# Key masks and row sums on ScalarE, four query loads on its queue, probabilities normalised later

## The chip, the cores and the metric

The kernel runs on one core of one Trainium2 chip. A core has TensorE (matrix products into PSUM), VectorE, ScalarE and GpSimd (all of which work on SBUF, and VectorE and ScalarE on PSUM too), and SyncE, whose queue issues most loads and stores; ScalarE's queue can issue them as well. The engines run side by side and wait for each other by semaphores; each works through its own queue in order. The metric is the time of one execution on the device, in microseconds (us), lower is better.

## What is computed

Three stages, the output of each being the input of the next. Inputs are fp32; q and k are drawn eight times as wide as written here.

```python
# 1. attention: B, H, S, D = 4, 8, 576, 64; keys and values are averaged in groups of 8 -> 72 of each
k_p = k.reshape(B, H, 72, 8, D).mean(axis=3)
v_p = v.reshape(B, H, 72, 8, D).mean(axis=3)
scores = matmul(q, k_p.T) / sqrt(D)
attn = exp(scores - max(scores));  attn = attn / (sum(attn) + 1e-9)
x = matmul(attn, v_p)                      # then (B, S, H*D) -> 2304 tokens x 512
# 2. four experts, each weighted by a token's probability
p = domain_probs / (domain_probs.sum(-1) + 1e-9)
x = sum over e of p[:, e] * (relu(x @ w1[e]) @ w2[e])      # 512 -> 1024 -> 512
# 3. gated layer
out = ((x @ g_w1) * (x @ g_w2) @ g_w3) @ g_wout            # 512 -> 1024 -> 1024 -> 512
```

## The kernel before

The 2304 tokens are cut into 18 query tiles of 128 rows (t = 0 to 17) and six blocks of three tiles. Products are split into a high and a low part (`hi_lo`, lines 178 to 180: ScalarE writes the rounded high part, another engine the remainder), and each product is three matmuls (`mm3`, line 173).

The program begins with a lead-in (list `lead`, lines 651 to 654): keys and values of the first batch are pooled, the first three query tiles scored, exponentiated, normalised, turned and attended, which gives the first block of x. Then expert 0 runs over all blocks in units of (block, 128 hidden columns), in `run_first` (line 1182): a unit's first product, and two units later its second. The rest of the attention is threaded between these units: `hooks[n]` is a list of pieces that is run in gap n, and a unit of the first block has two gaps (one behind its first product, one behind the second product of the unit two places back). The order of each engine's queue is the order in which the code writes its instructions (`manual_schedule`).

A tensor name in the rows is that of the tile: `ap` is the area of the attention's small tiles, `plain` another area (masked keys, probabilities), `stx...` are staging tiles of loads, `raw` weights as loaded, `w2h`/`w2l` an expert's second weights split, `g` the bank of a unit's product.

What the change touches:

- `load_k` (line 399) loads 128 pooled rows' worth of keys; chunks 1 and 3 of the first batch go through ScalarE's queue, all others through SyncE's.
- `pool_k` (line 411) sums each group of eight keys into `kp` and multiplies it by a mask of two columns (line 424) into `kb`, so that one product scores two heads. For the second batch (b = 1) chunks 0 to 3 are done by GpSimd in the lead-in (lines 421 to 424), chunk 4 by VectorE in gap 1. `make_kT` (line 433) turns `kb` on TensorE (line 438), in gaps 3 (chunks 0 to 2) and 4 (chunks 3 and 4); ScalarE evacuates (line 442).
- `load_qb` (line 473) loads a query tile from t = 3 on; a tile that lies in two batches, as t = 4 does, takes eight loads, four for each part (line 481). VectorE turns it (`make_qT`, line 499).
- `scores` (line 505) writes two banks per tile. From the end of the lead-in on, scores, turned keys and turned probabilities share two banks in turn (`spare[:2]`, line 1127).
- `exps` (line 517): VectorE takes the maximum (line 525); for t = 0, 1, 3, 4, 5 ScalarE does one exponential per head (line 528), eight for a tile, for the others VectorE subtracts first (line 530) and ScalarE does two (line 531).
- `sums` (line 534): VectorE sums the exponentials (line 537) and makes the reciprocal (lines 538, 539); `normalise` (line 541) multiplies, on GpSimd or VectorE. `attn_T` (line 544) turns the result on TensorE (line 551), ScalarE evacuates (line 557). `attend` (line 559) multiplies with the pooled values (line 566).
- `probs` (line 623) normalises the experts' probabilities on VectorE (lines 625 to 628), in gap 7; `turn_dp` (line 636) brings them into place, ScalarE evacuates (line 640); their first reader is `accumulate` (line 711), behind the first block's last unit.
- `Stream.fill` (lines 198, 200) issues the loads of weights on SyncE's queue.

The exponentials of t = 3 stand in gap 0, of t = 4 in gap 5, of t = 5 in gap 8, the turning of t = 3 in gap 7, of t = 4 in gap 10.

Of the kernel before, what the change touches and what calls it, by code (L numbers as in the profile page):

```python
# [8 lines left out]
F32 = mybir.dt.float32  # L9
F32R = mybir.dt.float32r  # L10
U32 = mybir.dt.uint32
AF = mybir.ActivationFunctionType
ALU = mybir.AluOpType
AX = mybir.AxisListType
# [3 lines left out]
def fused_kernel(  # L18
# [16 lines left out]
    nc = tc.nc  # L35
    PSUM = bass.MemoryType.PSUM

    B, H, S, D = q.shape
# [4 lines left out]
    P = 128  # L43
# [5 lines left out]
    TPB = BLK // P  # L49
# [6 lines left out]
    NCH = (NROW + P - 1) // P  # L56
# [4 lines left out]
    def segments(t0, n):  # L61
        done = 0
        while done < n:
            b, s = divmod(t0 + done, S)
            step = min(n - done, S - s)
            yield done, step, b, s
            done += step

    LAG = 2
    LEAD = 3  # L70
# [260 lines left out]
    with tc.manual_schedule():  # L331
# [3 lines left out]

        ap = Places(**packed(ap1, [
            ("at", (H // 2) * BLK * 4, 2), ("e", H * NK * 4, 3), ("kT", NCH * P * 4, 2), ("vp", H * D * 4, 2), ("qT", NP * P * 4, 1),
            ("kp", D * 4, 2), ("mx", H * 4, 2), ("sm", H * 4, 2), ("hm", NCH * H * 4, 1), ("mk", NCH * 2 * 4, 1),
            ("sp", NTILE * 4, 1)], 4 * XO),
            **packed(plain, [("kb", NCH * 2 * D * 4, 1)], PLAIN, WORK + XT))  # L340
        acc_d = dpool.tile([P, NTILE, DM], F32, tag="acc", name="acc")
# [11 lines left out]
        hm = ap.tile([P, NCH, H], F32, tag="hm", name="hm", bufs=1)  # L353
# [5 lines left out]
        mk = ap.tile([P, NCH, 2], F32, tag="mk", name="mk", bufs=1)  # L359
# [19 lines left out]
        def stage(*what):  # L379
            holds[what] = spots[kind_of(what)].pop(0)  # L380
            return holds[what]
# [15 lines left out]
        in_t, kb_t, kT_t, vp_t, qT_t, sc_t, e_t, sm_t, at_t = {}, {}, {}, {}, {}, {}, {}, {}, {}  # L397
# [13 lines left out]
        def pool_k(b, c, eng=nc.vector):  # L411
            if c == 0:
                kb_t[b] = ap.tile([P, NCH, 2, D], F32, tag="kb", name="kb", bufs=1)
            r, n = in_t.pop(("k", b, c))
            kp = ap.tile([P, D], F32, tag="kp", name="kp")
            if n < P and b == 0:
                nc.gpsimd.memset(kb_t[b][n:, c], 0.0)
            if eng is nc.vector:
                eng.tensor_reduce(kp[:n], r[:n, :].rearrange("p (r d) -> p d r", d=D), axis=AX.X, op=ALU.add)  # L419
            else:  # L420
                eng.tensor_tensor(r[:n, :256], r[:n, :256], r[:n, 256:], op=ALU.add)
                eng.tensor_tensor(r[:n, :128], r[:n, :128], r[:n, 128:256], op=ALU.add)
                eng.tensor_tensor(kp[:n], r[:n, :64], r[:n, 64:128], op=ALU.add)
            (eng if b == 1 else nc.gpsimd).tensor_tensor(kb_t[b][:n, c], kp[:n].unsqueeze(1).broadcast_to([n, 2, D]),
                                    mk[:n, c].unsqueeze(2).broadcast_to([n, 2, D]), op=ALU.mult)

# [2 lines left out]
        def turn_ident(pw, n):  # L429
            for _ in range(n):  # L430
                nc.tensor.transpose(pw[:, :P], ident, ident)

        def make_kT(b, g0, g1):
            if g0 == 0:
# [31 lines left out]
        def load_q(t):  # L466
# [3 lines left out]
                                  q[b, :, s:s + n, :].rearrange("h p d -> p h d"))  # L470
            in_t["q", t] = r

        def load_qb(t):

            r = stage("qb", t).rearrange("p x (h c) -> p (x h) c", c=4 * D)
            for off, n, b, s in segments(t * P, P):
                view = q[b].rearrange("(h g) (j a) d -> g j h (a d)", g=2, a=4)
                for g in range(2):
                    for m in range(2):
                        p0 = 64 * g + 32 * m + off // 4  # L480
                        nc.sync.dma_start(r[p0:p0 + n // 4, :, :7 * 32],
                                          view[g, s // 4:(s + n) // 4, :, 32 * m:32 * (m + 7)])
            in_t["qb", t] = r.rearrange("p h (a x) -> p h a x", a=4)[:, :, :, :32]

        def make_qT(t):
# [17 lines left out]
        G = H // 2  # L503
# [13 lines left out]
        def exps(t):  # L517
            e = ap.tile([P, H, NK], F32, tag="e", name="e", bufs=3)
            mx = ap.tile([P, H], F32, tag="mx", name="mx")
            for half, sc in enumerate(sc_t.pop(t)):  # L520
                s3 = sc[:, :2 * W].rearrange("p (g j) -> p g j", j=NK)
                m = mx[:, half * G:(half + 1) * G]
                eh = e[:, half * G:(half + 1) * G]
                alone = t < 2 * TPB and t != LEAD - 1
                nc.vector.tensor_reduce(m, s3, axis=AX.X, op=ALU.max, negate=alone)  # L525
                if alone:
                    for g in range(G):
                        nc.scalar.activation(eh[:, g], s3[:, g], AF.Exp, bias=m[:, g:g + 1])  # L528
                else:
                    nc.vector.tensor_tensor(eh, s3, m.unsqueeze(2).broadcast_to([P, G, NK]), op=ALU.subtract)  # L530
                    nc.scalar.activation(eh, eh, AF.Exp)
            e_t[t] = e

        def sums(t):

            sm_t[t] = ap.tile([P, H], F32, tag="sm", name="sm")
            nc.vector.tensor_reduce(sm_t[t], e_t[t], axis=AX.X, op=ALU.add)  # L537
            nc.vector.tensor_scalar(sm_t[t], sm_t[t], 1e-9, float(POOL), op0=ALU.add, op1=ALU.mult)
            nc.vector.reciprocal(sm_t[t], sm_t[t])

        def normalise(t, eng):
            eng.tensor_tensor(e_t[t], e_t[t], sm_t[t].unsqueeze(2).broadcast_to([P, H, NK]), op=ALU.mult)
# [62 lines left out]
        def do_qT(t):  # L605
            return [(("q" if t < LEAD else "qb", t), lambda: make_qT(t))] if t < NTILE else []

        def do_scores(t):
            return [(None, lambda: scores(t))]

        def do_exps(t):
            return [(None, lambda: exps(t))]

        def do_normalise(t, eng=nc.gpsimd):
            return [(None, lambda: sums(t)), (None, lambda: normalise(t, eng))]
# [18 lines left out]
        W0, W1 = 20, 22  # L634
# [7 lines left out]
        def warm(n):  # L642

            def f():
                warm_ps.append(bank("warm"))
                turn_ident(warm_ps[-1], n)
            return [(None, f)]

        k0, kT0, k1, kT1 = do_k(0), do_kT(0), do_k(1, 4), do_kT(1, 3)
        v0 = do_v(0, GP, GP, GP, GP, GP, VE)[:6] + [(None, lambda: pool_v_pe(0, 6))]  # L650
        lead = (warm(W0) + k0[:4] + kT0[:1] + k0[4:] + do_qT(0) + kT0[1:] + do_qT(1) + do_scores(0) + do_exps(0) + v0[:3]
                + do_qT(2) + do_scores(1) + do_exps(1) + do_scores(2) + do_normalise(0) + v0[3:4] + do_exps(2) + warm(W1) + [(None, turn_dp)]
                + v0[6:] + do_normalise(1) + v0[4:5] + weight(GP) + do_turn(0) + do_normalise(2, VE) + v0[5:6] + do_turn(1) + do_turn(2)
                + do_qT(3) + k1[:4] + do_attend(0) + weight(VE))

        hooks = [[] for _ in range(2 * FC * ATT_BLOCKS + 11)]
        hooks[1] = k1[4:]
        hooks[7] = [(None, probs)]
        hooks[2] = do_qT(TPB + 1)
        hooks[3] = kT1[:1]  # L660
        hooks[4] = kT1[1:]
# [855 lines left out]
```

## Time and profile before

| | us |
|---|---|
| three runs: median (lowest to highest) | 1151.28 (1150.27 to 1153.33) |
| the profiled execution, its own time | 1150.86 |
| its span in the trace, first to last instruction | 1149.1 |
| granted TensorE clock, mean | 1.000 |

Busy in the span: TensorE 99%, VectorE 69%, GpSimd 37%, ScalarE 32%. Times in the rows are us from the start of the span unless marked ns. A row of the timeline has start, length, engine, line of the code, operation, destination and sources, count, and in brackets how long the engine stood idle before it and what it then waited for. The ends of matmuls are modelled, since they are pipelined. Where an instruction waits for several others, the trace names the one that it takes for the last.

### The profile page before, as it was taken

The page shows a single profiled execution, that of the slowest core. Times are in us where ns is not written, and L with a number is a line of the kernel's source. Part 1 is how long each engine was busy: PE and PEld are TensorE (multiplying, and loading weights), DVE is VectorE, ACT ScalarE, POOL GpSimd, SP SyncE. Part 2 cuts the span into 40 slices and gives each one's busy share as a digit, 9 for nine tenths or more (in the row PEclk, how much of TensorE's full clock was granted, in tenths as well). Part 3 has the DMA queues.
Part 4 walks back from the last instruction along what each step waited for, and adds up shares of the span by engine and source line. Part 5 has one row for each costly group of instructions (what it writes and reads, how often), then busy time and mean ns, then how long its engine had stood idle before and what let it go on. Part 6 is the DMA issues. An engine that isn't in the chain of part 4 may idle for free.

```text
span 1149.1 us, 17172 instructions
## 1 busy us (share of the span) xinstructions
PE 1141.3 (99%) x5995; PEld 1033.7 (90%) x5995; DVE 797.4 (69%) x1458; ACT 371.5 (32%) x633; POOL 421.9 (37%) x390
## 2 busy tenths in 40 slices
PE   9999999999999999999999999999999999999998
PEld 7898888999989898989898989989889999999997
DVE  7876553867768598658679678877786675774554
ACT  5543433345413053504134421305353223230110
POOL 6874212424616166534436652515000111331211
PEclk9999999999999999999999999999999999999999
DMA  9955525345875825495944678785485175947341
GB/s 215 235 136 133 170 80 202 142 175 179 299 246 171 259 79 162 138 313 171 271 151 125 192 224 193 240 210 140 151 198 230 35 267 202 336 153 283 116 164 55
DMA packets 211473, 213.85 MB, mean 186 GB/s; under 512 B 86569, under 2 KB 166697, under 8 KB 211387
## 3 DMA queue, kind: packets, MB, share of 16 engines
q1 hardware_dynamic: 211099, 212.23, 59.3%
q8 instruction: 47, 0.77, 0.3%
q10 hardware_dynamic: 288, 0.52, 0.1%
q14 instruction: 39, 0.32, 0.1%
HBM read 140.87 MB, written 71.83 MB: 185 GB/s over the span
## 4 chain that ended last, share of the span: by engine, by line
PE 96%; DMA 2%; DVE 1%; ACT 0%; POOL 0%; issue 0%; SPq 0%; ACTq 0%; DVEq 0%; POOLq 0%
PE g L176 18%; PE g L174 18%; PE g L175 18%; PE s L176 13%; PE s L175 13%; PE s L174 13%; PE x_ps L566 1%; PE sc L512 1%; PE at_ps L551 1%; DMA stxl<-in_moe_w_dram 1%; DMA stxl<-in_k_dram 1%; DMA stxl<-in_q_dram 0%; DVE ap L419 0%; DVE ap L525 0%; DVE ap L537 0%; ACT ap L528 0%
## 5 line engine op out<-in xcount | busy, mean ns | idle before, releaser
L972 DVE TENSOR_TENSOR plain<-s,plain 128x384 f32<-128x384 f32 x300 | 158.4, 554 | 81.0 <-ACT plain L976 33.5
L180 POOL TENSOR_TENSOR round<-x5l,round 128x768 fp32r<-128x768 f32 x60 | 112.2, 1871 | 271.6 <-ACT round L179 254.6
L176 PE MATMUL s<-xo,wl 128*128 128x384 f32 x624 | 208.8, 335 | 0.0
L174 PE MATMUL s<-xo,wh 128*128 128x384 f32 x624 | 208.8, 335 | 0.0
L175 PE MATMUL s<-xo,wh 128*128 128x384 f32 x624 | 208.8, 335 | 0.0
L174 PE MATMUL g<-w2l,round 128*128 128x512 f32 x522 | 205.1, 393 | 0.8 <-POOL w2l L180 0.8
L176 PE MATMUL g<-w2h,round 128*128 128x512 f32 x522 | 204.0, 391 | 0.0
L175 PE MATMUL g<-w2h,round 128*128 128x512 f32 x522 | 203.8, 390 | 0.0
L174 PEld LDWEIGHTS s<-xo,wh 128*128 128x128 f32 x624 | 117.2, 188 | 0.5
L175 PEld LDWEIGHTS s<-xo,wh 128*128 128x128 f32 x624 | 117.2, 188 | 0.5
L176 PEld LDWEIGHTS s<-xo,wl 128*128 128x128 f32 x624 | 117.2, 188 | 0.0
L174 PEld LDWEIGHTS g<-w2l,round 128*128 128x128 f32 x522 | 98.1, 188 | 21.1 <-POOL w2l L180 1.1
L176 PEld LDWEIGHTS g<-w2h,round 128*128 128x128 f32 x522 | 98.0, 188 | 20.7
L175 PEld LDWEIGHTS g<-w2h,round 128*128 128x128 f32 x522 | 98.1, 188 | 19.4
L292 POOL TENSOR_TENSOR x5l<-x5l,x5h 128x256 uint32<-128x256 uint32 x80 | 60.4, 754 | 138.5 <-DVE x5h L291 133.0
L976 ACT ACTIVATE plain<-s 128x384 f32<-128x384 f32 x60 | 29.2, 487 | 230.9 <-PE s L176 195.2
L179 ACT ACTIVATE round<-x5l 128x768 fp32r<-128x768 f32 x60 | 50.9, 848 | 147.7 <-DVE x5l L1377 146.5
L180 POOL TENSOR_TENSOR round<-plain,round 128x768 fp32r<-128x768 f32 (+1 forms) x29 | 52.4, 1808 | 116.2 <-ACT round L179 65.4
L286 DVE TENSOR_SCALAR x5l<-x5h 128x256 uint32<-128x256 uint32 x80 | 51.9, 649 | 54.8 <-DMA gate<-x5l 30.9
L972 DVE TENSOR_TENSOR x5l<-s,plain 128x384 f32<-128x384 f32 x120 | 65.5, 555 | 23.6 <-PE s L176 17.0
L1215 ACT ACTIVATE plain<-plain 128x768 f32<-128x768 f32 x36 | 30.5, 849 | 112.7 <-DVE plain L972 112.7
L704 DVE SCALAR_TENSOR_TENSOR round<-g,round 128x384 fp32r<-128x384 f32 x48 | 26.4, 551 | 58.1 <-ACT round L703 58.0
(255 smaller groups left out, 2254.2 us busy)
## 6 DMA issues: line engine op xcount, KB each, us to landing
xo<-keptx SPq DMA_DIRECT2D x42, 768.0 KB
raw<-in_moe_w_dram SPq DMA_DIRECT2D x54, 256.0 KB
keptx<-xo SPq DMA_DIRECT2D x12, 768.0 KB
x5h<-in_moe_w_dram SPq DMA_DIRECT2D x128, 64.0 KB
x5h<-in_moe_w_dram SPq DMA_DIRECT2D x32, 256.0 KB
ob<-acc SPq DMA_DIRECT2D x24, 256.0 KB
kept<-xo SPq DMA_DIRECT2D x8, 768.0 KB
xo<-kept SPq DMA_DIRECT2D x8, 768.0 KB
```

Source lines behind the costliest of these rows:

```text
L174: nc.tensor.matmul(ps, lh, rl, start=first, stop=False)
L175: nc.tensor.matmul(ps, lh, rh, start=False, stop=False)
L176: nc.tensor.matmul(ps, ll, rh, start=False, stop=last)
L179: nc.scalar.activation(hi, src, AF.Copy)
L180: (lo_eng or nc.vector).tensor_tensor(lo, src, hi.bitcast(F32), op=ALU.subtract)
L286: nc.vector.tensor_scalar(au, h, 0x7FFFFFFF, None, op0=ALU.bitwise_and)
L292: nc.gpsimd.tensor_tensor(au, au, l, op=ALU.add)
L512: nc.tensor.matmul(sc[off:off + n, (hp % 2) * W:(hp % 2 + 1) * W], qT[:, hp, off:off + n], kT_t[b][:, hp * W:(hp + 1) * W], start=True, st ...
L704: nc.vector.scalar_tensor_tensor(hl, ps, 0.0, hh.bitcast(F32), op0=ALU.max, op1=ALU.subtract)
L972: nc.vector.tensor_tensor(to, one, two, op=ALU.add)
L976: nc.scalar.activation(x, product(j, A11, B11), AF.Copy)
L1215: nc.scalar.activation(r, r, AF.Relu)
```

## The change

ScalarE multiplies the first three chunks of the second batch's keys by their masks (six activations of 128x64 in gap 0, ahead of the scores of t = 3), in place of three multiplications by GpSimd; the pooled keys get four places instead of two. For t = 3, 4, 5 each exponential also writes its row sum (`accum_out`), and `sums` leaves VectorE's sum out; the sums get three places instead of two. Four of the eight loads of query tile 4, those of its second part, are issued from ScalarE's queue, behind the exponentials of t = 2 in the lead-in. `probs` moves from gap 7 to gap 13.

```diff
@@ -335,7 +335,7 @@
 
         ap = Places(**packed(ap1, [
             ("at", (H // 2) * BLK * 4, 2), ("e", H * NK * 4, 3), ("kT", NCH * P * 4, 2), ("vp", H * D * 4, 2), ("qT", NP * P * 4, 1),
-            ("kp", D * 4, 2), ("mx", H * 4, 2), ("sm", H * 4, 2), ("hm", NCH * H * 4, 1), ("mk", NCH * 2 * 4, 1),
+            ("kp", D * 4, 4), ("mx", H * 4, 2), ("sm", H * 4, 3), ("hm", NCH * H * 4, 1), ("mk", NCH * 2 * 4, 1),
             ("sp", NTILE * 4, 1)], 4 * XO),
             **packed(plain, [("kb", NCH * 2 * D * 4, 1)], PLAIN, WORK + XT))
         acc_d = dpool.tile([P, NTILE, DM], F32, tag="acc", name="acc")
@@ -421,6 +421,9 @@
                 eng.tensor_tensor(r[:n, :256], r[:n, :256], r[:n, 256:], op=ALU.add)
                 eng.tensor_tensor(r[:n, :128], r[:n, :128], r[:n, 128:256], op=ALU.add)
                 eng.tensor_tensor(kp[:n], r[:n, :64], r[:n, 64:128], op=ALU.add)
+            if b == 1 and c < NCH - 2:
+                kp_t[c] = kp
+                return
             (eng if b == 1 else nc.gpsimd).tensor_tensor(kb_t[b][:n, c], kp[:n].unsqueeze(1).broadcast_to([n, 2, D]),
                                     mk[:n, c].unsqueeze(2).broadcast_to([n, 2, D]), op=ALU.mult)
 
@@ -429,6 +432,12 @@
         def turn_ident(pw, n):
             for _ in range(n):
                 nc.tensor.transpose(pw[:, :P], ident, ident)
+
+        kp_t = {}
+
+        def mask_k(c):
+            for a in range(2):
+                nc.scalar.activation(kb_t[1][:, c, a], kp_t[c], AF.Copy, scale=mk[:, c, a:a + 1])
 
         def make_kT(b, g0, g1):
             if g0 == 0:
@@ -470,16 +479,25 @@
                                   q[b, :, s:s + n, :].rearrange("h p d -> p h d"))
             in_t["q", t] = r
 
+        rest_of_q = []
+
         def load_qb(t):
 
             r = stage("qb", t).rearrange("p x (h c) -> p (x h) c", c=4 * D)
-            for off, n, b, s in segments(t * P, P):
+
+            def part(eng, off, n, b, s):
                 view = q[b].rearrange("(h g) (j a) d -> g j h (a d)", g=2, a=4)
                 for g in range(2):
                     for m in range(2):
                         p0 = 64 * g + 32 * m + off // 4
-                        nc.sync.dma_start(r[p0:p0 + n // 4, :, :7 * 32],
-                                          view[g, s // 4:(s + n) // 4, :, 32 * m:32 * (m + 7)])
+                        eng.dma_start(r[p0:p0 + n // 4, :, :7 * 32],
+                                      view[g, s // 4:(s + n) // 4, :, 32 * m:32 * (m + 7)])
+
+            for k, seg in enumerate(segments(t * P, P)):
+                if k and t == TPB + 1:
+                    rest_of_q.append(lambda seg=seg: part(nc.scalar, *seg))
+                else:
+                    part(nc.sync, *seg)
             in_t["qb", t] = r.rearrange("p h (a x) -> p h a x", a=4)[:, :, :, :32]
 
         def make_qT(t):
@@ -524,8 +542,11 @@
                 alone = t < 2 * TPB and t != LEAD - 1
                 nc.vector.tensor_reduce(m, s3, axis=AX.X, op=ALU.max, negate=alone)
                 if alone:
+                    if t >= LEAD and half == 0:
+                        sm_t[t] = ap.tile([P, H], F32, tag="sm", name="sm")
                     for g in range(G):
-                        nc.scalar.activation(eh[:, g], s3[:, g], AF.Exp, bias=m[:, g:g + 1])
+                        more = dict(accum_out=sm_t[t][:, half * G + g:half * G + g + 1]) if t >= LEAD else {}
+                        nc.scalar.activation(eh[:, g], s3[:, g], AF.Exp, bias=m[:, g:g + 1], **more)
                 else:
                     nc.vector.tensor_tensor(eh, s3, m.unsqueeze(2).broadcast_to([P, G, NK]), op=ALU.subtract)
                     nc.scalar.activation(eh, eh, AF.Exp)
@@ -533,8 +554,9 @@
 
         def sums(t):
 
-            sm_t[t] = ap.tile([P, H], F32, tag="sm", name="sm")
-            nc.vector.tensor_reduce(sm_t[t], e_t[t], axis=AX.X, op=ALU.add)
+            if t not in sm_t:
+                sm_t[t] = ap.tile([P, H], F32, tag="sm", name="sm")
+                nc.vector.tensor_reduce(sm_t[t], e_t[t], axis=AX.X, op=ALU.add)
             nc.vector.tensor_scalar(sm_t[t], sm_t[t], 1e-9, float(POOL), op0=ALU.add, op1=ALU.mult)
             nc.vector.reciprocal(sm_t[t], sm_t[t])
 
@@ -649,13 +671,15 @@
         k0, kT0, k1, kT1 = do_k(0), do_kT(0), do_k(1, 4), do_kT(1, 3)
         v0 = do_v(0, GP, GP, GP, GP, GP, VE)[:6] + [(None, lambda: pool_v_pe(0, 6))]
         lead = (warm(W0) + k0[:4] + kT0[:1] + k0[4:] + do_qT(0) + kT0[1:] + do_qT(1) + do_scores(0) + do_exps(0) + v0[:3]
-                + do_qT(2) + do_scores(1) + do_exps(1) + do_scores(2) + do_normalise(0) + v0[3:4] + do_exps(2) + warm(W1) + [(None, turn_dp)]
+                + do_qT(2) + do_scores(1) + do_exps(1) + do_scores(2) + do_normalise(0) + v0[3:4] + do_exps(2) + [(None, lambda: rest_of_q.pop()())]
+                + warm(W1) + [(None, turn_dp)]
                 + v0[6:] + do_normalise(1) + v0[4:5] + weight(GP) + do_turn(0) + do_normalise(2, VE) + v0[5:6] + do_turn(1) + do_turn(2)
                 + do_qT(3) + k1[:4] + do_attend(0) + weight(VE))
 
         hooks = [[] for _ in range(2 * FC * ATT_BLOCKS + 11)]
         hooks[1] = k1[4:]
-        hooks[7] = [(None, probs)]
+        hooks[0] = [(None, lambda c=c: mask_k(c)) for c in range(NCH - 2)]
+        hooks[13] = [(None, probs)]
         hooks[2] = do_qT(TPB + 1)
         hooks[3] = kT1[:1]
         hooks[4] = kT1[1:]
```

## Rows read from the trace of the kernel before

**Rows 1.** The page: busy time of each engine, share of the span, instructions
```profile
PE 1141.3 (99%) x5995; PEld 1033.7 (90%) x5995; DVE 797.4 (69%) x1458; ACT 371.5 (32%) x633; POOL 421.9 (37%) x390
```
**Rows 2.** TensorE's waits over the span: total us, times, longest us
```profile
PE warm L431 <- POOL ident masks.py:199: 1.4, 1, 1.4
...
PE at_ps L551 <- POOL ap L542: 0.3, 1, 0.3
```
**Rows 3.** Timeline of TensorE, 22 to 52 us
```profile
22.40 2.80 PE L566 MATMUL x_ps<-ap 72*64 72x384 f32 x16 [0.34 <-ACT ap L557]
...
30.95 0.52 PE L438 MATMUL kT_ps<-ident,plain 128*128 128x128 f32 x3 [0.40 <-POOL plain L424]
...
34.62 0.50 PE L174 MATMUL g<-w2l,round 128*128 128x512 f32 x1 [0.83 <-POOL w2l L180]
...
50.98 0.63 PE L551 MATMUL at_ps<-ident,ap 128*72 128x128 f32 x4 [0.36 <-ACT ap L528]
51.83 0.63 PE L551 MATMUL at_ps<-ident,ap 128*72 128x128 f32 x4 [0.21 <-ACT ap L528]
```
**Rows 4.** Timeline of GpSimd, 30 to 35 us
```profile
30.22 0.40 POOL L424 TENSOR_TENSOR plain<-ap 128x128 f32<-128x128 f32 x1
...
32.83 1.74 POOL L180 TENSOR_TENSOR w2l<-raw,w2h 128x512 fp32r<-128x512 f32 x1
```
**Rows 5.** Timeline of ScalarE, 28 to 52 us (the x4 row from a shorter stretch)
```profile
28.43 0.62 ACT L179 ACTIVATE w2h<-raw 128x512 fp32r<-128x512 f32 x1
29.89 0.96 ACT L528 ACTIVATE ap<-sc,ap 128x72 f32<-128x72 f32 x4 [0.84 <-DVE ap L525]
...
49.98 1.80 ACT L528 ACTIVATE ap<-sc,ap 128x72 f32<-128x72 f32 x8 [2.90 <-DVE ap L525]
```
**Rows 6.** Timeline of VectorE, 43 to 64 us
```profile
43.69 0.68 DVE L537 TENSOR_REDUCE ap<-ap 128x8 f32<-128x576 f32 x1
...
45.19 0.18 DVE L625 TENSOR_REDUCE ap<-plain 128x18 f32<-128x72 f32 x1
...
45.92 1.36 DVE L628 TENSOR_TENSOR plain<-plain,ap 128x72 f32<-128x72 f32 x1
...
63.30 0.56 DVE L704 SCALAR_TENSOR_TENSOR round<-g,round 128x384 fp32r<-128x384 f32 x1 [2.00 <-ACT round L703]
```
**Rows 7.** SyncE's queue, 18 to 28 us: timeline, then waits of 24 to 28
```profile
18.47 0.33 SPq L403 DMA_DIRECT2D stxl<-in_k_dram  x1
...
21.19 0.33 SPq L481 DMA_DIRECT2D stxl<-in_q_dram  x1
...
22.09 0.37 SPq L481 DMA_DIRECT2D stxl<-in_q_dram  x1
...
27.71 0.31 SPq L481 DMA_DIRECT2D stxl<-in_q_dram  x1
...
SPq L481 <- DMA raw<-in_moe_w_dram: 2.1, 2, 1.2
SPq L481 <- DMA stxl<-in_k_dram: 1.0, 1, 1.0
```
**Rows 8.** ScalarE and its queue, 1 to 23 us
```profile
1.25 0.45 ACTq L403 DMA_DIRECT2D stxl<-in_k_dram  x1
...
16.39 0.44 ACT L531 ACTIVATE ap<-ap 128x288 f32<-128x288 f32 x1 [0.42 <-DVE ap L530]
...
19.00 0.27 ACT L464 ACTIVATE ap<-vp_ps 72x128 f32<-72x128 f32 x1 [1.60 <-PE vp_ps L460]
...
19.69 2.66 ACT L557 ACTIVATE ap<-at_ps 72x512 f32<-72x512 f32 x5
```
**Rows 9.** TensorE's warm-up transposes; then the windows view: engines' busy us, PEclk, DMA
```profile
1.43 4.53 PE L431 MATMUL warm<-ident 128*128 128x128 f32 x20 [1.43 <-POOL ident masks.py:199]
...
13.91 2.57 PE L431 MATMUL warm<-ident 128*128 128x128 f32 x22
...
22.00:25.00 3.00, 2.66 (x17) 1.06 (x16) 2.82 (x4) 1.73 (x4) 2.84 (x5) 1.00 0.99 233
```

## The prediction

> **What bounds the kernel now.** I read the page's first part first [rows 1]: TensorE is busy 1141.3 of 1149.1 us, so only an edit that shortens or lengthens one of its waits counts. Its waits over the whole run are six kinds and 4.5 us together, of which the first and the last stand in [rows 2]; none lies behind 52 us. The timeline of TensorE gives the places that the change can touch [rows 3]: 0.40 us at 30.95 (the second batch's keys, "kT_ps"), 0.83 at 34.62 (the low part of an expert's weights, from GpSimd), 0.36 and 0.21 at 50.98 and 51.83 (turning the fifth query's probabilities). They are 1.80 us, 0.16%. Since nothing waits later, what these first 60 us give or take arrives at the end whole. The sum is made against the profiled execution, 1150.86 us, of which 1149.1 is the span; the median of the three runs lies 0.42 above it, and I add the differences to that median, 1151.28. About 0.3% (3.5 us) is what a measurement of this kernel can tell from no change.
>
> **The key masks.** GpSimd loses three of its four masks of the second batch, 0.40 us each; the instructions there stand without a gap, and behind them starts the low part of the weights (1.74 us at 32.83), 0.05 us after whose end TensorE goes on [rows 3, 4]. It starts 1.1 us earlier, so the wait of 0.83 goes. ScalarE gains six small activations (128x64) in front of the fourth query's exponentials. Nearest row: the exponentials, 128x72 with a per-partition operand as the masks have: four in 0.96 us, eight in 1.80, so 0.21 apart [rows 5]. Six cost 1.28. By the Trainium skill's page "ScalarE: Activation LUTs" (What ACT_TABLE_LOAD costs) such an instruction takes 186 ns, 93 more for a pointer operand and 0.833 ns a column, less 93 ns of overlap: an estimate from that page of 0.24 each and 1.44 for six, with which the forecast would be 0.16 us higher; the row stands. ScalarE is free from about 28.96 (its weight split of 28.43 runs to 29.05 and the next instruction overlaps by 0.1), so the masks end at 30.24. The exponentials start at 29.89 today: 0.35 us later. The third key sum, ready before the mask of 30.22 today and two masks earlier then, doesn't hold the last mask.
>
> This matters because the wait at 30.95 is named wrongly. GpSimd's mask was done at 30.62 [rows 4], and a release by GpSimd takes 0.05, so TensorE would have gone on at 30.67. What ends at 30.85 is the fourth exponential [rows 5]: the transposes write the bank that the scores left, so they follow the first four exponentials. The masks lengthen this wait.
>
> **Row sums by ScalarE.** Twenty-four exponentials (queries four to six) also sum. Before shows no such instruction. Bounds: nothing, if the sum comes with the pass; one more small instruction each, 0.21 us, if it is written out separately. Reading one column is less work than 72; I take 0.1. The first four add 0.4 us to the wait at 30.95 (0 to 0.85). VectorE loses three sums of about 0.7 us, that of 43.69 one of them [rows 6].
> The two waits together: TensorE is free for the weights at 33.79 (34.62 less 0.83), 2.84 us after the keys' transposes begin [rows 3]. It now arrives at 30.95+0.35+0.4+2.84 = 34.54 and goes on at once, where it went on at 34.62: 0.1 us gained (0.5 to -0.4).
>
> **Probabilities normalised six places on.** VectorE's four instructions from 45.19 to 47.28 (first and last in [rows 6]) and the sum at 43.69 leave the stretch ahead of the sixth query's maximum: 2.7 us. That maximum releases the exponentials at 49.98, before which ScalarE stood 2.90 us [rows 5], and they free the two banks that TensorE waits for at 50.98 and 51.83 [rows 3]. Starting near 47.3, eight with 0.1 more each end near 50; TensorE asks for the second bank at 51.62. Both waits go, 0.57; half of it if VectorE's remaining order holds the maximum. In the new place VectorE stands 2.00 us before 63.30 [rows 6], and the four took 2.09: hidden but for a tenth, and nothing of TensorE waits for that. If the cover were gone, the remainder of an activation would come 2 us late, which TensorE reads two units on.
>
> **Four loads from ScalarE's queue.** SyncE's eight loads of the fifth query take 0.31 us each, but the last is issued only at 27.71, 6.5 us after the first [rows 7]: one of them waits 1.0 us for keys to land, two 2.1 us for weights. Those are the keys issued at 18.47 and the two weights issued behind them, each eight places before the load that waits; the other issues fit the same count. ScalarE's own first loads, 0.41 and 0.45 us (the second in [rows 8]), are counted among SyncE's; they stood in front and waited for nothing. So a load placed on ScalarE's queue behind 16.83 (its exponentials of the third query [rows 8]) makes ScalarE wait for a landing. In order behind it stand the scale of the experts' probabilities, the pooled values (19.00), a weight split and five evacuations back to back from 19.69 to 22.35, the last of which releases TensorE at 22.40 [rows 3, 8].
> Which landings? No row says how the four are numbered among SyncE's loads. If they take the next four numbers, the last waits for the landing behind SyncE's issue of 18.47, is out at 18.9, and costs at most 0.2. If they alternate with SyncE's, as two queues that both wait would, the last waits for the landing behind 21.19 or the one behind 22.09 [rows 7]. With its issue (0.45) and one small activation (0.21) the pooled values start at 21.85 to 22.75 instead of 19.00: 2.9 to 3.8 us, all passed on, since the evacuations have no slack. I take alternation and, since ScalarE asks for its first number before SyncE's next key load is out, 3.1. SyncE's freed time feeds no wait of TensorE: no load is among its releasers [rows 2, 3].
>
> **Sum.** +3.1 for the loads, -0.1 for masks and sums, -0.6 for the probabilities: +2.4 us. Forecast 1151.28 + 2.4 = **1153.7 us**, slower by 0.2%, within what counts as the same.
>
> **Rivals.**
> (a) The loads don't hold ScalarE: numbered in a row, or their landings past. Then a loss of 0 to 0.2 and a gain of 0.2 to 1.1: about 1150.5. For it: ScalarE comes at 16.83, before SyncE's queue is as late as it gets. Against it: every SyncE issue from 18.47 to 27.71 in [rows 7] stands on a landing.
> (b) The other side: the four are counted behind the keys and the two weights that the code asks for earlier. Then the last waits for the landing behind 27.71, ScalarE is free at 28.2, the pooled values start 9.4 us late, and the time is 1151.28+9.4-0.7 = 1160.0 us. It decides from the point where the last issue on ScalarE's queue comes after about 22.7 (a loss of 4.2 less 0.7). Against it: at 16.83 SyncE itself has not yet issued the keys of 18.47.
> (c) The clock. TensorE would stand some 3.4 us before 25.5. The granted clock reads 1.00 there [rows 9], the 2.4 GHz level; at the start 20 warm-up transposes took 4.53 us, later 22 took 2.57, which is the ratio of the two levels. If it falls, a few us of work take twice as long: 2 to 3 us more, 1156.2. The Trainium skill's page "TensorE: Matmul & The Clock Gate" (Part 1) says that an idle TensorE goes back to the lower level; no run here shows it within the kernel.
> (d) The change doesn't do what it says: the sums cost a full instruction, the masks more than the row, and the wait at 30.95 grows by more than the weights' wait gives. That is the dear end of the range.
>
> **How the numbers follow.** Forecast (alternation, with d) 56%, of which 8 points end beyond +3.5; (a) 28%, of which 2 points below -3.5; (b) 6%; (c) 5%; unforeseen 5%: 1 faster, 2 same, 2 slower. Slower 8+6+4+2 = 20%, faster 3%, same 77%. Low end: (a) with free sums, -1.1, restarts of TensorE that the modelled ends hide, -0.5, and 0.3 of scatter: 1149.4. High end: 3.8, sums dear (+0.4), half of the probabilities' gain (-0.3): +3.9, so 1155.2. (b), (c) and most of the unforeseen lie outside.
>
> **What would show it.** Right: the pooled values' row on ScalarE at 21.8 to 22.8 with four issues ahead, the last just after a landing; x_ps at 25.2 to 26.2; kT_ps waiting about 1.1; no wait for w2l; none at the fifth query's at_ps; VectorE's four rows near 64 with no one waiting. Wrong: pooled values at 19.0 (a), ScalarE free only near 28 (b), a granted clock under 1.00 behind 25 (c), exponentials still 0.21 apart or over 0.4 (d), or a load among TensorE's releasers.

## The result and the profile after

The changed kernel takes 1157.58 us (median of 6 runs, 1155.21 to 1157.90), the kernel before, run beside it, 1151.04 (6 runs, 1149.73 to 1153.33). The ratio is 1.0051, with a 95% interval of 1.0037 to 1.0064: slower by 6.5 us, where 2.4 were forecast, and above the stated range (1149.4 to 1155.2). The profiled execution took 1157.85, its span is 1156.1 (1149.1 before).

The page's first part, busy time of each engine, answers to [rows 1]:

```profile
PE 1144.6 (99%) x5995; PEld 1036.0 (90%) x5995; DVE 791.9 (69%) x1455; ACT 374.5 (32%) x663; POOL 419.1 (36%) x387
```

TensorE's waits over the span (total us, times, longest us) answer to [rows 2]:

```profile
PE x_ps L588 <- ACT ap L579: 4.4, 1, 4.4
...
PE kT_ps L447 <- POOL plain L427: 1.3, 5, 0.3
PE kT_ps L447 <- ACT ap L549: 1.1, 1, 1.1
```

Of the waits before, those for the low part of the weights (w2l, 0.83) and at the fifth query's turning (at_ps, 0.57) are gone. The one ahead of x_ps, 0.34 before, has grown to 4.4. The timeline of TensorE, 20 to 70 us, answers to [rows 3]:

```profile
26.29 5.39 PE L588 MATMUL x_ps<-ap 72*64 72x384 f32 x16 [4.42 <-ACT ap L579]
...
35.61 1.30 PE L530 MATMUL sc<-ap 128*128 128x144 f32 x8
...
40.06 0.55 PE L447 MATMUL kT_ps<-ident,plain 128*128 128x128 f32 x3 [1.06 <-ACT ap L549]
...
44.91 1.20 PE L530 MATMUL sc<-ap 128*64 128x144 f32 x16
...
58.44 1.04 PE L573 MATMUL at_ps<-ident,ap 128*72 128x128 f32 x8
...
66.56 1.04 PE L573 MATMUL at_ps<-ident,ap 128*72 128x128 f32 x8
```

x_ps starts at 26.29 instead of 22.40, and its 16 products take 5.39 us instead of 2.80. What stood ahead of it on ScalarE answers to [rows 8]:

```profile
16.42 6.45 ACTq L493 DMA_DIRECT2D stxl<-in_q_dram  x4
22.91 0.30 ACT L662 ACTIVATE plain<-warm 128x72 f32<-128x72 f32 x1 [6.06 <-DMA stxl<-in_q_dram]
23.04 0.27 ACT L473 ACTIVATE ap<-vp_ps 72x128 f32<-72x128 f32 x1
...
23.72 2.52 ACT L579 ACTIVATE ap<-at_ps 72x512 f32<-72x512 f32 x5
```

The four issues lie at 16.42, 18.53, 21.31 and 22.55, and ScalarE does nothing else until 22.91. The pooled values start at 23.04 instead of 19.00, the five evacuations at 23.72 instead of 19.69. The chain of work that ended last, 14 to 27 us (start, length, what), shows why the second issue comes at 18.53:

```profile
11.72 6.79 DMA raw<-in_moe_w_dram
...
18.53 4.35 DMA stxl<-in_q_dram
```

It waits for weights that SyncE issued at 11.72, eight loads before it in the count of both queues together. The fourth issue, 22.55, follows the landing at 22.52 of the keys that SyncE issued at 16.02, again eight loads before it. The semaphores in the trace confirm both: the loads tell of their landings on eight of them in turn, numbers 100 to 107; the second issue waits for 102, which the weights of 11.72 signal, and the fourth for 100, which the keys of 16.02 signal. SyncE's issues meanwhile (the two of the second row start at 17.54 and 19.02):

```profile
16.02 0.35 SPq L403 DMA_DIRECT2D stxl<-in_k_dram  x1
17.54 1.81 SPq L403 DMA_DIRECT2D stxh<-in_k_dram  x2
19.58 0.48 SPq L403 DMA_DIRECT2D stxl<-in_k_dram  x1
21.81 0.38 SPq L200 DMA_DIRECT2D raw<-in_moe_w_dram  x1
```

The row at 22.91 names the landing of a load as what ScalarE waited for. But here and in e2, e4, e9, e10 and e11 ScalarE goes on 0.04 to 0.05 us after the end of its last issue (22.87 here), whatever landed then; it is that issue which frees it.

The windows view (busy us of PE, PEld, DVE, ACT and POOL with their counts, then granted clock, share of the DMA engines, GB/s) answers to the last row of [rows 9]:

```profile
22.00:25.00 3.00, 0.00 (x0) 0.00 (x0) 1.59 (x2) 2.09 (x6) 1.10 (x1) 1.00 1.00 273
25.00:26.00 1.00, 0.00 (x0) 0.00 (x0) 0.00 (x0) 1.00 (x3) 0.92 (x3) 0.84 1.02 200
26.00:30.00 4.00, 3.71 (x12) 1.48 (x14) 0.87 (x2) 1.22 (x3) 3.61 (x9) 0.50 0.80 156
...
36.00:40.00 4.00, 3.00 (x20) 2.68 (x18) 3.18 (x6) 4.00 (x18) 1.29 (x1) 1.00 0.97 280
```

TensorE has stood since about 21.9; its clock falls from 1.00 to 0.50, the 1.2 GHz level, between 25 and 26, and is back at 1.00 behind 36.

To see where the 7.0 us of span came in, take the starts of six instructions of TensorE and subtract those of before: x_ps (22.40), the fourth query's scores (27.32), the second batch's keys (30.95), the fifth query's scores (36.91), its turning (50.98), and the sixth query's turning (59.55). What a column adds to the one on its left was lost, or won, between them. The starts are those of one profiled execution of each kernel; medians and ratios are of all its runs.

| kernel | x_ps | scores 4 | keys | scores 5 | turning 5 | turning 6 | median us | ratio to before (95%) |
|---|---|---|---|---|---|---|---|---|
| after | 3.89 | 8.29 | 9.11 | 8.00 | 7.46 | 7.01 | 1157.58 | 1.0051 (1.0037 to 1.0064) |
| e1, no loads moved | 0.12 | 0.14 | 0.92 | -0.15 | -0.70 | -0.47 | 1150.97 | 0.9998 (0.9988 to 1.0007) |
| e2, loads alone | 3.57 | 7.85 | 7.89 | 6.73 | 6.18 | 5.74 | 1156.13 | 1.0039 (1.0024 to 1.0054) |
| e10, loads, probabilities | 4.24 | 7.48 | 7.30 | 6.17 | 5.63 | 5.18 | 1156.27 | 1.0042 (1.0027 to 1.0057) |
| e11, all, clock held | 3.22 | 3.22 | 4.00 | 2.91 | 2.37 | 1.92 | 1154.43 | 1.0029 (1.0018 to 1.0039) |
| e9, loads alone, clock held | 3.63 | 3.63 | 3.46 | 2.35 | 1.80 | 1.36 | 1153.56 | 1.0022 (1.0013 to 1.0031) |
| e7, masks alone | 0.37 | 0.37 | 0.78 | -0.28 | -0.17 | -0.17 | 1149.96 | 0.9996 (0.9986 to 1.0005) |
| e6, probabilities alone | 0.10 | 0.12 | 0.10 | -0.45 | -0.97 | 0.36 | 1151.10 | 1.0002 (0.9993 to 1.0011) |

The kernel before had medians of 1151.58 (beside e1 to e4), 1150.89 (e5 to e8) and 1150.81 (e9 to e11).

In the changed kernel, then, 3.89 us are ScalarE's hold, 4.40 the clock, 0.82 the keys' turning, and 1.11, 0.54 and 0.45 come back. These last are the waits of before at w2l (0.83 in the waits view) and at the fifth query's turning (0.36 and 0.21): in starts a wait is worth 0.2 to 0.3 us more than the view shows, since the modelled ends of the matmuls ahead of it reach into it. Behind 66.56 the difference stays at 7.0.

### The profile page after: what moved, and what is told of

Read it like the earlier page. It is cut to its first block, busy times and chain, and to the rows that moved or that the text cites. A ratio compares the mean times of both kernels' runs of the same rounds, so it can differ in the third digit from the quotient of the medians.

```text
span 1156.1 us, 17189 instructions
## 1 busy us (share of the span) xinstructions
PE 1144.6 (99%) x5995; PEld 1036.0 (90%) x5995; DVE 791.9 (69%) x1455; ACT 374.5 (32%) x663; POOL 419.1 (36%) x387
## 4 chain that ended last, share of the span: by engine, by line
PE 97%; DMA 1%; ACT 1%; SPq 1%; issue 0%; DVE 0%
PE g L176 18%; PE g L174 18%; PE g L175 18%; PE s L174 13%; PE s L176 13%; PE s L175 13%; PE x_ps L588 2%; PE sc L530 1%; PE at_ps L573 1%; DMA raw<-in_moe_w_dram 1%; DMA stxl<-in_q_dram 0%; SPq L478 0%; DMA stxl<-in_v_dram 0%; ACT ap L579 0%; PE kT_ps L447 0%; SPq L403 0%
## 5 line engine op out<-in xcount | busy, mean ns | idle before, releaser
L174 PE MATMUL g<-xl,round 128*128 128x384 f32 x192 | 67.0, 349 | 0.0
```

The costliest lines, as they stand in the source:

```text
L174: nc.tensor.matmul(ps, lh, rl, start=first, stop=False)
```

## The experiments

**The theory.** ScalarE is held by its loads; TensorE stands for it; the clock falls, which costs about as much again; masks, sums and probabilities don't matter beside that. **The rivals.** Masks and sums carry a part; the clock is only a sign of the hold; issuing from ScalarE's queue is dear in itself; and, as the prediction summed it, the parts add up. The edits are shown shortened: `...` stands for the rest of a line, and unchanged lines are left out.

**e1, all eight loads on SyncE's queue**, the rest as changed.

```diff
-                if k and t == TPB + 1:
+                if False:
-  ... + do_exps(2) + [(None, lambda: rest_of_q.pop()())] + warm(W1) ...
+  ... + do_exps(2) + warm(W1) ...
```

> The changed kernel with all eight loads of the fifth query on SyncE's queue again; masks, row sums and the later probabilities stay. If the loads are the whole loss (by holding ScalarE and by the clock that falls behind it), x_ps starts at 22.4 with 16 products in 2.80 us, the granted clock stays at 1.00, the keys' turning waits about 1.2 us, no wait for w2l and none at the fifth query's at_ps, and the time is 0.4 to 1.1 us under the kernel before: about 1150.3. If masks and sums carry a part of the 6.5 us, it stays above the kernel before, by up to 3 us.

1150.97 us, no loss left. Timeline of TensorE:

```profile
31.87 0.55 PE L447 MATMUL kT_ps<-ident,plain 128*128 128x128 f32 x3 [1.18 <-ACT ap L549]
...
50.28 1.04 PE L573 MATMUL at_ps<-ident,ap 128*72 128x128 f32 x8
...
53.86 1.22 PE L530 MATMUL sc<-ap 128*128 128x144 f32 x8 [0.47 <-DVE ap L560]
```

Masks and sums lengthen the keys' wait to 1.18, and the waits for w2l and at the fifth query are gone, as forecast. A new one of 0.47 at the sixth query's scores, behind a transposition by VectorE whose load landed late, costs 0.68 in starts: it takes back the 0.45 won at the second of the fifth query's waits, and 0.23 more. The three parts together win 0.5 us at the sixth query's turning, too little for the medians.

**e2, the four loads alone**: the kernel before with the changed `load_qb` and the piece in the lead-in, nothing else.

```diff
+                if k and t == TPB + 1:
+                    rest_of_q.append(lambda seg=seg: part(nc.scalar, *seg))
+  ... + do_exps(2) + [(None, lambda: rest_of_q.pop()())] ...
```

> The kernel before with only the four loads moved to ScalarE's queue. If the loads are the whole loss: x_ps starts near 26.3 after a wait of 4.4 us, the clock reads 0.5 for about 10 us behind it, the wait for w2l goes and the waits at at_ps (0.57 together) stay, and the time is about 1158, 7 us above the kernel before. If masks and sums carry a part, it is under 1156.

1156.13 us: the loads by themselves, hold and clock both, make 4.6 of the 6.5 us (5.74 of 7.01 at the sixth query's turning in the traces).

```profile
25.97 5.26 PE L575 MATMUL x_ps<-ap 72*64 72x384 f32 x16 [3.75 <-ACT ap L566]
...
38.84 0.49 PE L438 MATMUL kT_ps<-ident,plain 128*128 128x128 f32 x3
...
57.16 1.03 PE L560 MATMUL at_ps<-ident,ap 128*72 128x128 f32 x8
```

But two points of the expectation miss. The waits at 51 and 52 don't stay: the eight transposes at 57.16 run on without one, though neither sums nor probabilities were moved here. And the kernel is not as slow as the changed one, so masks and sums carry a part; the intervals of the two ratios overlap, and e9 to e11 below settle its size.

**e3, TensorE kept at work by transposes.** 36 transposes of the identity, into the bank of the warm-up, ahead of x_ps.

```diff
-  ... + do_qT(3) + k1[:4] + do_attend(0) + weight(VE))
+  ... + do_qT(3) + k1[:4] + [(None, lambda: turn_ident(warm_ps[-1], 36))] + do_attend(0) + weight(VE))
```

> The changed kernel with 36 transposes of the identity into a spare bank put ahead of the first block's x_ps, so that TensorE works while ScalarE is held (36 at 0.117 us each, 4.2 us). If the clock is a cause of its own: x_ps still starts near 26.3, but the clock reads 1.00 and its 16 products take 2.80 us in place of 5.39; the time is 4.4 us under the changed kernel, about 1153.5. If the lower clock costs nothing that the hold has not cost already, the time stays at 1157.6 or rises.

1156.64 us (ratio 1.0046, 1.0031 to 1.0061), because the edit was badly placed:

```profile
24.46 4.15 PE L434 MATMUL warm<-ident 128*128 128x128 f32 x36 [1.84 <-ACT plain L662]
28.54 2.80 PE L588 MATMUL x_ps<-ap 72*64 72x384 f32 x16
```

The bank still held the experts' probabilities, which ScalarE evacuates behind its loads, so the transposes waited for the hold themselves and then delayed x_ps to 28.54. The run says nothing on the cost of the clock. It shows that a stand of 1.84 us left the clock at 1.00.

**e4, two of the four loads on ScalarE's queue**, two on SyncE's.

```diff
-            def part(eng, off, n, b, s):
+            def part(eng, off, n, b, s, gs=range(2)):
-                for g in range(2):
+                for g in gs:
-                    rest_of_q.append(lambda seg=seg: part(nc.scalar, *seg))
+                    part(nc.sync, *seg, gs=[0])
+                    rest_of_q.append(lambda seg=seg: part(nc.scalar, *seg, gs=[1]))
```

> The changed kernel with two of the four loads on ScalarE's queue and the other two back on SyncE's. If ScalarE is held only because a load waits for the landing of the load eight places before: the second of the two then waits for the keys issued at about 14.5, which land near 18.5, ScalarE is free at about 18.9, x_ps starts at 22.4 to 22.6, the clock stays at 1.00 and the time is that of the kernel with all loads on SyncE's queue, about 1150.5. If an issue from ScalarE's queue is dear in itself, half of the delay stays: x_ps near 24.3 and about 3 us above the kernel before.

1150.31 us, ratio 0.9993 (0.9984 to 1.0002): half of the loads cost nothing. Timelines of ScalarE and of TensorE:

```profile
16.43 2.61 ACTq L493 DMA_DIRECT2D stxl<-in_q_dram  x2
19.09 0.30 ACT L663 ACTIVATE plain<-warm 128x72 f32<-128x72 f32 x1 [2.22 <-PE vp_ps L469]
19.22 0.28 ACT L473 ACTIVATE ap<-vp_ps 72x128 f32<-72x128 f32 x1
```

```profile
22.47 2.80 PE L589 MATMUL x_ps<-ap 72*64 72x384 f32 x16 [0.38 <-ACT ap L580]
...
32.92 0.90 PE L447 MATMUL kT_ps<-ident,plain 128*128 128x128 f32 x3 [2.30 <-ACT ap L550]
```

ScalarE is free at 19.09, just in time for the pooled values (19.22), whose products end there anyway. So the issues are not dear; which landing the last one waits for decides. Here it was issued at 18.72, behind the landing of the weights of 11.92 (not of keys, as the expectation had it): the place of the changed kernel's second load. The profiled execution, 1152.30, is the longest of the ten: its weights landed late, so that ScalarE's exponentials and with them the keys' turning came late (2.30 us), and the clock fell for a short time, as the windows show:

```profile
30.00:34.00 4.00, 1.70 (x9) 1.38 (x8) 2.13 (x5) 4.00 (x24) 2.35 (x4) 0.86 0.76 236
34.00:38.00 4.00, 4.00 (x18) 3.83 (x17) 2.95 (x6) 2.73 (x7) 2.09 (x2) 0.71 0.93 248
```

Taken microsecond by microsecond, the clock reads 0.50 from 33 to 36.

**e5 and e11, the transposes in a free bank.** e5 writes 30 transposes to the bank that VectorE empties; e11 has 20.

```diff
                 nc.vector.tensor_copy(dst, src)
+                last_at.append(pt)
-  ... + do_qT(3) + k1[:4] + do_attend(0) + weight(VE))
+  ... + do_qT(3) + k1[:4] + [(None, lambda: turn_ident(last_at[0], 30))] + do_attend(0) + weight(VE))
```

> The changed kernel with 30 transposes of the identity ahead of the first block's x_ps, now written to the bank that VectorE empties (free near 22.6), so that they don't wait for the held ScalarE; at 0.115 us each they last 3.5 us and end before 26.3. If the lower clock is a loss of its own beside the hold: x_ps starts at 26.0 to 26.6 as in the changed kernel, its 16 products take 2.80 us in place of 5.39, the clock reads 1.00 throughout, and the time is 4.4 us under the changed kernel, about 1153.5 (2.0 to 2.5 above the kernel before). If the clock is only a sign of the hold, the time stays near 1157.6.

1154.83 us, ratio 1.0037 (1.0024 to 1.0051); the clock reads 1.00 throughout. The 30 transposes last longer than the hold, whose last evacuation ends at 25.64 here:

```profile
23.33 3.49 PE L434 MATMUL at_ps<-ident 128*128 128x128 f32 x30 [0.78 <-DVE ap L577]
26.75 2.80 PE L589 MATMUL x_ps<-ap 72*64 72x384 f32 x16
```

> The changed kernel with 20 transposes ahead of x_ps in place of the 30 of the run before, which lasted 1.06 us longer than ScalarE held x_ps. If the clock's part is settled: the clock reads 1.00, x_ps starts when ScalarE's fifth evacuation ends, 25.6 to 26.3, and the time is 0.5 to 1 us under that of 30 transposes, near 1154.0, which is 3.5 us under the changed kernel. If a stand of 0.5 to 1 us behind the transposes is enough for the clock to fall, 1157.

1154.43 us, 3.2 under the changed kernel (2.9 if each is taken over the kernel before that ran beside it). Timeline of TensorE, then two windows:

```profile
22.70 2.40 PE L434 MATMUL at_ps<-ident 128*128 128x128 f32 x20 [0.78 <-DVE ap L577]
25.62 2.80 PE L589 MATMUL x_ps<-ap 72*64 72x384 f32 x16 [0.52 <-ACT ap L580]
...
34.95 0.55 PE L447 MATMUL kT_ps<-ident,plain 128*128 128x128 f32 x3 [1.18 <-ACT ap L549]
```

```profile
25.00:29.00 4.00, 3.48 (x21) 1.71 (x21) 1.68 (x4) 2.57 (x7) 3.56 (x8) 1.00 0.82 144
29.00:36.00 7.00, 5.82 (x37) 5.50 (x36) 4.77 (x8) 5.74 (x27) 3.81 (x6) 1.00 0.73 220
```

x_ps waits for ScalarE as in the changed kernel, but its products take 2.80 us. In the table e11 adds nothing between x_ps and the fourth scores, where the changed kernel adds 4.40. The clock is a loss of its own: 4.4 us between these two traces, 2.9 between the medians (the two intervals, 1.0037 to 1.0064 and 1.0018 to 1.0039, just touch; e10 below has a cleaner pair). What stays, 3.6 us over the kernel before (2.1 to 4.5 by the interval), holds the 2.4 that were forecast without the clock.

**e9, the loads alone, with 20 transposes**: e2 with e11's edit. It asks whether the hold adds to the other waits or takes their place.

> The kernel before with only the four loads on ScalarE's queue, and 20 transposes of the identity (0.115 us each, 2.3 us together) ahead of the first block's x_ps, which keep TensorE at work for a part of the hold. x_ps then starts when ScalarE releases it, 25.6 to 26.3 against 22.40, and the clock stays at 1.00. If the hold adds to what the other waits cost (as the prediction summed it), the time is 3.3 to 3.9 us above the kernel before, near 1154.6. If the hold takes the place of the later waits (0.40 at the keys, 0.83 at w2l, 0.57 at the fifth query, 1.80 together, since the other engines catch up meanwhile), it is 1.5 to 2.1 us above it, near 1152.8, and those waits are gone.

1153.56 us, 2.75 above the kernel before; by the interval 1.5 to 3.6, which leaves both open, so the trace must decide:

```profile
26.03 2.80 PE L576 MATMUL x_ps<-ap 72*64 72x384 f32 x16 [0.91 <-ACT ap L567]
...
34.41 0.52 PE L438 MATMUL kT_ps<-ident,plain 128*128 128x128 f32 x3 [0.23 <-issue]
...
52.78 1.03 PE L560 MATMUL at_ps<-ident,ap 128*72 128x128 f32 x8
```

No wait for w2l, none at the fifth query's turning, and the keys' wait is 0.23. Of 3.63 us at x_ps 1.36 are left at the sixth query's turning. The gains on the way, 1.11 at w2l and 0.55 and 0.44 behind it, are the changed kernel's, in a kernel without masks, sums or later probabilities. So the hold takes the place of those waits. Some 0.8 us of the span's 2.2 come later; 0.5 of them is one wait for VectorE between 900 and 1000 us that before doesn't show (e11 has it too, 0.6). Why it comes is open.

**e10, loads and probabilities**: e2 with `probs` in gap 13.

> The changed kernel without masks and row sums: the four loads on ScalarE's queue and the probabilities six places on. If the delay has already taken the place of the waits at 51 and 52, the later probabilities win nothing here and the time is that of the loads alone, 1156.1, that is 1 to 1.5 us under the changed kernel, whose keys' turning waits 1.06 us more for masks and sums; if the parts add up, it is 0.5 us above the changed kernel less the masks' part, near 1157.5.

1156.27 us, as e2: the later probabilities win nothing here.

```profile
26.64 4.80 PE L575 MATMUL x_ps<-ap 72*64 72x384 f32 x16 [4.70 <-ACT ap L566]
...
38.25 0.52 PE L438 MATMUL kT_ps<-ident,plain 128*128 128x128 f32 x3 [0.22 <-issue]
```

The keys' wait is 0.22, where the changed kernel, with masks and sums, has 1.06. That and e11 against e9 (0.78 against -0.17 between the fourth scores and the keys) put masks and sums at about 1 us of loss once TensorE is late. So the rival that they carry a part is right, for about 1 of the 6.5 us.

The pair e10 and e9, run beside each other, also prices the clock: e10's four runs lie between 1156.01 and 1156.55 at a mean clock of 0.995 to 0.997, e9's ten between 1152.77 and 1154.13 at 1.00. They differ by the 20 transposes and by the probabilities, which alone show no gain (e6).

**e6, probabilities alone.**

```diff
-        hooks[7] = [(None, probs)]
+        hooks[13] = [(None, probs)]
```

> The kernel before with the probabilities normalised six places on, and nothing else. If the four instructions on VectorE held the sixth query's maximum: no wait of TensorE at the turning of the fifth query near 51 and 52 (0.36 and 0.21 before), the waits for the keys' turning (0.40) and for w2l (0.83) stay, about 0.6 us less than before. If VectorE's sum of the fourth query had to go too, half of the 0.57 stays.

```profile
50.01 1.34 PE L551 MATMUL at_ps<-ident,ap 128*72 128x128 f32 x8
...
54.65 1.22 PE L512 MATMUL sc<-ap 128*128 128x144 f32 x8 [1.22 <-DVE ap L499]
```

The two waits go without the sums' help. But the sixth query's scores then wait 1.22 for VectorE's transposition, whose load landed late; the median, 1151.10, shows no gain. In this trace the wait for w2l, which the edit doesn't touch and which was expected to stay, is 0.28 instead of 0.83. So a wait differs by half a microsecond between executions, and a gain of that size at w2l, read from one trace, can't be put down to an edit. That this wait is gone in e2, e9 and e10, none of which moves the masks, rests on three traces.

**e7, masks alone**: only the edits of `kp`, `pool_k`, `mask_k` and `hooks[0]`.

> The kernel before with the six masks on ScalarE, and nothing else. If the keys' turning waits for the fourth exponential (the bank), the wait at 30.95 grows by the masks' time, from 0.40 to 0.8 to 0.95, and the wait for w2l goes: 0.3 to 0.45 us less in sum. If it waits for GpSimd's last mask, as the trace names it, it shrinks to nothing and 1.2 us are won.

```profile
31.73 0.55 PE L447 MATMUL kT_ps<-ident,plain 128*128 128x128 f32 x3 [0.82 <-ACT ap L537]
```

The keys' wait grows to 0.82, so it hangs on the fourth exponential, not on GpSimd's mask; the wait for w2l is gone. From x_ps to the fifth scores 0.65 us are won in the trace, more than the 0.3 to 0.45 expected, since the wait at w2l is worth 1.06 in starts against 0.41 lost at the keys; the time, 1149.96, can't be told from that of before.

**e8, two masks and the probabilities** on the kernel before (`c < 2` in e7's edit, and e6's), as an attempt at a faster kernel.

> The kernel before with two of the second batch's key masks on ScalarE (four activations, 0.24 apart, of which 0.84 us fit into ScalarE's idle time ahead of the fourth query's exponentials) and the probabilities six places on; no row sums, no loads on ScalarE's queue. Expected: the keys' turning waits 0.5 to 0.6 us (0.40 before), w2l at most 0.1 (0.83 before), no wait at the fifth query's turning (0.57 before): 1.1 to 1.2 us under the kernel before, a ratio of 0.9990. If something late takes the place of these waits, no difference.

```profile
36.57 1.20 PE L521 MATMUL sc<-ap 128*64 128x144 f32 x16 [0.52 <-DVE ap L508]
...
55.01 1.22 PE L521 MATMUL sc<-ap 128*128 128x144 f32 x8 [1.30 <-DVE ap L508]
```

1151.37 us, ratio 1.0000 (0.9991 to 1.0009). The old waits shrink or go (0.35 at the keys, none for w2l, 0.21 at the fifth query), and waits for the transpositions of the fifth and the sixth query take their place (0.52 and 1.30). None of these kernels is shown to beat the kernel before.

## Why the prediction was wrong

**The loads: the mechanism was right, the size low.** Each load behind the landing of the one eight places before, ScalarE held: as worked out. But the two queues did not take strict turns. Among ScalarE's four issues SyncE put four of its own (17.54, 19.02, 19.58, 21.81), so the last waited for the landing of the first of the second batch's keys, the later of the two landings that the prediction named (that behind 22.09). Its dear end, 3.8 us, was the one to take, not 3.1; x_ps came 3.89 later, and 3.22 to 4.24 in the other kernels of the table with four loads on that queue. The pooled values start at 23.04, 0.29 behind the late end of the forecast's span.

**The clock: the step that failed.** The forecast's sum has a term for the time that TensorE stands and none for the clock behind it. Rival (c) came about, and on top of the forecast: 4.40 us in the trace, 2.9 between the medians. It was given 5%, with the remark that no run showed the clock fall within the kernel. But the longest wait of TensorE in [rows 2] is 1.4 us, so that trace could not show what a stand of 3 us does; and [rows 9] showed both levels, 4.53 us for 20 transposes at the start, before TensorE had worked, and 2.57 for 22 later. The forecast made the stand itself, at three chances in five, and the clock's chance hung on it alone. The price of 2 to 3 us fits the medians, each over its own kernel before (2.9 changed kernel less e11, 2.7 e10 less e9, 1.8 e2 less e9), and is low for the profiled executions (4.40 in the changed kernel, 4.28 in e2, 3.24 in e10). The Trainium skill's page "TensorE: Matmul & The Clock Gate" (Part 1) says that an idle TensorE goes back to the lower level; the traces agree, within the kernel: 0.50 behind stands of 3.75 to 4.70 us, and for some 3 us behind one of 2.30 (e4).

**Masks and sums: the parts right, their sum not.** The masks lie 0.24 apart, not 0.21. The prediction's estimate from the Trainium skill's page "ScalarE: Activation LUTs" (What ACT_TABLE_LOAD costs), 0.24, agrees with this trace. The exponentials lie 0.29 to 0.30 apart, so the sum costs 0.09 (0.1 taken), though it is an instruction of its own, 0.19 long:

```profile
37.28 1.53 ACT L440 ACTIVATE plain<-ap 128x64 f32<-128x64 f32 x6
38.72 0.30 ACT L549 ACTIVATE ap<-sc,ap 128x72 f32<-128x72 f32 x1
38.92 0.19 ACT L549 ACTIVATION_READ_ACCUMULATOR ap<-sc,ap 128x1 f32 x1
39.01 0.31 ACT L549 ACTIVATE ap<-sc,ap 128x72 f32<-128x72 f32 x1
```

The keys' turning loses 0.78 to 0.82 (0.75 forecast). Against that stood 0.83 at w2l, and in e1 the two more than balance: 0.78 lost at the keys, 1.07 won behind them. In the held kernel the other engines have caught up, w2l waits for nothing, and the loss stands alone.

**The probabilities: the same fault.** That the two waits go was right; up to the fifth query's turning alone 0.55 is won in e1 and 0.52 in e6. But the hold had already taken them (e9, e10), and without the hold a new wait at the sixth query's scores takes much of the gain back (e1) or more than all of it (e6). The prediction did not look for a wait behind the two that it removed. The new place is free, as said: VectorE's four rows lie between 67.74 and 69.22, with 1.08 us idle behind them, and no wait of TensorE names them.

**The sum.** +3.1 - 0.1 - 0.6 added terms from one trace as if each kept its worth when TensorE comes 3 us later. Measured at the sixth query's turning: 3.89 hold, 4.40 clock, 0.82 keys, and -2.10 that the delay gives back by itself (2.10 in e9 too, without masks, sums or later probabilities). Without the clock that is +2.61, close to the forecast's +2.4, but by luck: the hold came out 0.8 above its term, masks and sums at +0.82 instead of -0.1, and what comes back at 2.10 instead of 0.6, and not through the edit.

**The other rivals.** (a), no hold, is what e4 shows for two loads, not for four. (b) fell: ScalarE was free at 22.9, not 28.2. Of (d), the dear instructions hardly came (0.24 for a mask, 0.09 for a sum), but its outcome came by another way: the keys lose 0.82, and the weights' wait gives nothing that the delay would not have given.

**The signs named.** The keys' wait near 1.1 (1.06), no wait for w2l and none at the fifth query's turning were there; x_ps (26.29 for 25.2 to 26.2) and the pooled values (23.04 for 21.8 to 22.8) came just behind their spans. The sign against, a clock under 1.00 behind 25, was there too.

## What to carry to other kernels

In this kernel a load on ScalarE's queue made ScalarE wait for the landing of the load eight places before; before moving a load to a compute engine's queue, look up which landing that is, and what stands behind the load in that queue. If the stand of TensorE that comes of it is several us (here 3.75 to 4.70, and once 2.30), count the clock as part of the same event, not as a separate mishap. And a delay can fill waits further on, as here those at w2l and at the fifth query: gains at such waits can't be added to it.

## What was not expected of the hardware

How long TensorE stood and what the clock did: 1.84 us (e3), 1.00 throughout; 2.30 (e4), the clock at 0.86 and 0.71 in the two windows from 30 and 34 us; 3.75 (e2), 4.42 (after) and 4.70 (e10), a stretch at 0.50 in which x_ps took 5.26, 5.39 and 4.80 us in place of 2.80. The lower level lasted about 10 us in the changed kernel and in e2, 7 in e10 and 3 in e4; in e2 and e10 it set in only after x_ps had begun, by about 0.2 and 0.6 us. The loss differs between executions of one kernel (mean clock 0.995 to 0.997 over the changed kernel's runs).
